# A two-layer linear-attention and MLP kernel: q and k of a token tile as one product of 1280 columns, G in two wide parts, block moves a tile ahead

## The chip, the core and the metric

The kernel runs on one core of one Trainium2 chip, in one launch. The metric is the device time of that launch in microseconds (us), the median of several runs. The engines named below are TensorE (PE in the profile; its weight loads are PEld), VectorE (DVE), ScalarE (ACT), GpSimd (POOL) and SyncE (SP, which issues the transfers).

## The reference

All data are float32: 2048 tokens of 640 features, 32 heads of 20. Two layers with the same weights follow each other; each is a linear attention block and an MLP block with squared relu (640 to 1728 to 640).

```python
def _A_ref(x, wqkv, wo):
    qkv = (x @ wqkv).reshape(B, S, 3, H, Dh).transpose(2, 0, 3, 1, 4)
    q, k, v = qkv[0], qkv[1], qkv[2]
    phi = lambda t: jnp.where(t > 0, t + 1, jnp.exp(t)) + 1e-6
    pq, pk = phi(q), phi(k)
    kv = jnp.einsum("bhsd,bhse->bhde", pk, v)
    z = jnp.einsum("bhsd->bhd", pk)
    num = jnp.einsum("bhqd,bhde->bhqe", pq, kv)
    den = jnp.einsum("bhqd,bhd->bhq", pq, z)[..., None] + 1e-6
    return (num / den).transpose(0, 2, 1, 3).reshape(B, S, D) @ wo

x = x + _A_ref(_layernorm(x), A_wqkv, A_wo)
x = x + _B_ref(_layernorm(x), B_w1, B_b1, B_w2, B_b2)   # h = relu(x w1 + b1)^2; h w2 + b2
# and both lines once more
```

## The kernel before

Tokens are handled in 16 tiles of 128 (NT = 16). Features are cut into five chunks of 128 (DC = 5). A product in float32 accuracy is made of three matmuls (`mm3`): each operand is kept as a rounded high half and a low half, and high x low, low x high and high x high are added in PSUM. `split` makes the halves: ScalarE copies the high half (an operation of 640 columns), VectorE subtracts for the low half.

The attention block of a layer first runs a loop over the 16 token tiles. v is never formed: instead G = x^T phi(k), a 640 x 640 sum over all tokens, is collected, and the kv of the heads follows as wv^T G. For tile t the loop does this:

- `proj(psk, ...)` makes k: for each of five feature chunks and each half of the 640 columns three matmuls of 320 columns, 30 in all. q is made in the same way (`q_psum`).
- the statistics and the normalisation of tile t + 2 (`a_stats`, `a_apply`; VectorE, with two small GpSimd operations), then `blocks_T`, a VectorE transpose within 32 x 32 blocks, into y.
- `blocks_move`: 16 ScalarE copies of 32 x 160 move the blocks of y into z, which is the transposed tile; `xT_split` makes the halves of z. TensorE needs them for the next tile's k.
- `phi_psum`: ScalarE's exp and relu out of PSUM; `phi_sum`: VectorE's min and add. For k the result r is split (`kh`) and GpSimd adds it to acc. The normalised tile is split as well (`xh`). For q the result is stored to DRAM by `q_store` at the start of the next tile.
- `g_chunk`: G of two tiles at a time, five chunks of twelve matmuls of 320 columns. Two or three chunks stand in each tile; VectorE adds each from PSUM into G.

In layer 0 the loop also splits two blocks of MLP weights a tile (`prep.split`: ScalarE the high half, GpSimd the low half), and loads and stores them. Three tiles, LATE = (6, 10, 14), skip their q, so that q runs three tiles behind at the end; the last three q are made later, among the work that leads to the MLP. The order on every engine is the order in which the program is written. PSUM is a ring of four slots of two banks (`ps2`), shared by k, q, G and transposes.

After the loop comes the joint: `psz` (the column sums acc, spread to all partitions by a product with ones), the last pair's G, wv^T G (`pskv`, masked into `kvbd` by VectorE), its product with wo (`psM`), and the first attention outputs (`pso`). VectorE prepares phi(q) of the first tiles between them: `b_den`, `b_blocks`. The MLP follows, with the attention outputs of later tiles worked in.

Of the kernel before, what the change touches and what calls it, by code (L numbers as in the profile page):

```python
# [35 lines left out]
LATE = (6, 10, 14)  # L36
N_WARM, N_WARM_2 = 30, 15
F_BUFS = 12
# [10 lines left out]
def kernel(  # L49
# [37 lines left out]
    def ftile(name):  # L87
        return tmp.tile([P, D], F32, tag="f", name=name, bufs=F_BUFS)

# [296 lines left out]
    for layer in range(N_LAYERS):  # L386
# [12 lines left out]
        pa = ExitStack()  # L399
        pp = pa.enter_context(  # L400
            tc.tile_pool(name=f"ap_{layer}", bufs=4, space=bass.MemoryType.PSUM, reuse_waits="tile")
        )

        ring = [0, 1, 2, 3]

        def ps2(name, hold=False):

            i = ring.pop(0)
            if not hold:
                ring.append(i)  # L410
            return pp.tile([P, 1024], F32, tag=f"p{i}", name=name, bufs=1)

        G = ap.tile([P, DC, D], F32, name="G", tag="G", bufs=1)
# [3 lines left out]
        def phi_psum(ps, rtile=None):  # L417

            e = ftile("e")
            nc.scalar.activation(halves_sb(e), halves(ps), AF.Exp)  # L420
            r = rtile or ap.tile([P, D], F32, tag="r", name="r", bufs=3)
            nc.scalar.activation(halves_sb(r), halves(ps), AF.Relu)
            return e, r

# [13 lines left out]
        def g_chunk(p, c):  # L438
            ps = ps2("psG")
            for t in (2 * p, 2 * p + 1):  # L440
                xs = xh[t][:, :, c * P : (c + 1) * P]
                for j in range(2):
                    s = slice(j * HD, (j + 1) * HD)
                    mm3(
                        ps[:, j * 512 : j * 512 + HD], xs[:, 0], xs[:, 1],
                        kh[t][:, 0, s], kh[t][:, 1, s], t % 2 == 0, t % 2 == 1,
                    )
            g = halves_sb(G[:, c])
            if p == 0:
                nc.vector.tensor_copy(g, halves(ps))  # L450
            else:
                nc.vector.tensor_tensor(out=g, in0=halves(ps), in1=g, op=ALU.add)  # L452

        def q_psum(t, hold=False):
            ps = ps2("psq", hold)
            proj(ps, xT[t], wk("q"))
            return ps

        def q_post(t, ps):
            e, r = phi_psum(ps)  # L460
            phi_sum(e, r)
            rq[t] = r
# [5 lines left out]
        if layer == 0:  # L468

            psw = ps2("psw", hold=True)  # L470

            def warm(n):
                for _ in range(n):
                    nc.tensor.transpose(psw[:, :P], ident, ident)
# [8 lines left out]
            a_trans(0, ps2("psT"))  # L483
# [7 lines left out]
            ring.append(0)  # L491
# [92 lines left out]
        n_q = 0  # L584
        for t in range(NT):
            q_store(n_q - 1)
            a_load(t + 3, src)
            if t == 0 and layer == 0:
# [9 lines left out]
            psk = ps2("psk")  # L598
            proj(psk, xT[t], wk("k"))
            if t + 1 in yza:  # L600
                blocks_move(yza[t + 1], range(4) if t in LATE else (0, 1))
            elif t < 2 and layer == 0:
                if t == 0:
                    psq = ps2("psq")
                    proj(psq, xT[t], wk("q"), range(3))
                a_trans(t + 1, ps2("psT"))
                if t == 0:
                    proj(psq, xT[t], wk("q"), range(3, DC))
            early = t == 0 and layer > 0
            if not early:  # L610
                a_stats(t + 2)
            first = t == 0 and layer == 0
            if first:
                a_apply(t + 2)
            if t in LATE:
                xT_split(t + 1, yza.pop(t + 1)[1])
            e, r = phi_psum(psk)
            if first:
                eq, rq[t] = phi_psum(psq)
            phi_sum(e, r)  # L620
            if t >= 2:
                for c in ((0, 1) if t % 2 == 0 else (3, 4)):
                    g_chunk((t - 2) // 2, c)
            if t + 1 in yza:
                blocks_move(yza[t + 1], (2, 3))
# [4 lines left out]
            kh[t] = split_new(r, "kh")  # L630
            if t == 0:
                nc.gpsimd.tensor_copy(acc, r)
            else:
                nc.gpsimd.tensor_tensor(out=acc, in0=acc, in1=r, op=ALU.add)
            if not first and not early:
                a_apply(t + 2)
            if t + 2 < NT and not first and not early:
                yza[t + 2] = blocks_T(xt[t + 2])
            if t not in LATE:
                if not first:  # L640
                    psq = q_psum(n_q)
                if layer == 0:
                    first_loads.step(1 if t else 0, 1)
                if first:
                    phi_sum(eq, rq[t])
                else:
                    q_post(n_q, psq)
                n_q += 1
            if layer == 0 and t >= 1:
                if t > 1 and t not in LATE:  # L650
                    prep.split()
                    prep.split()
                if t + 1 not in LATE:
                    prep.load()
                    prep.load()
            if t >= 2 and t % 2 == 0:
                g_chunk((t - 2) // 2, 2)
        q_store(n_q - 1)


        psz = ps2("psz")
# [7 lines left out]
        b_den(0)  # L669
        b_blocks(0)  # L670
        blocks_move(yzp[0], range(4))
        for c in range(DC):
            g_chunk(NT // 2 - 1, c)
            if c == 1:
                b_den(1)
                b_blocks(1)
            if c == 3:
                b_den(2)
        b_split(0, xtile("pT"))
        blocks_move(yzp[1], range(3))  # L680
        psq = q_psum(NT - 3, hold=True)
        q_slot = ({0, 1, 2, 3} - set(ring)).pop()

# [8 lines left out]
        for c in range(NH):  # L692
            n = head_rows(c)
            ps = ps2("pskv")
            for d in range(DC):
                nc.tensor.matmul(  # L696
                    ps[:n, :n], vo["v", d][:, HR * c : HR * c + n], G[:, d, HR * c : HR * c + n],
                    start=d == 0, stop=d == DC - 1,
                )
            nc.vector.tensor_tensor(  # L700
                out=kvbd[c][:n, P : P + n], in0=ps[:n, :n], in1=maskf[:n, :n], op=ALU.mult
            )
            if c == 0:
                blocks_move(yzp[1], (3,))
                e, rl = phi_psum(psq)
                b_load_pq(3)
            if c == 1:
                b_div(2)
                b_load_x(0)
            if c == 2:  # L710
                yzp[2] = blocks_T(pq.pop(2))
            if c == 3:
                b_split(1, xtile("pT"))
                b_load_x(1)
            if c == NH - 1:
                phi_sum(e, rl)
                nc.sync.dma_start(pqd[NT - 3], rl)
                ring.append(q_slot)
# [62 lines left out]
        proj(psq, xT[NT - 2], wk("q"))  # L781
# [6 lines left out]
        proj(psq, xT[NT - 1], wk("q"))  # L788
        phi_sum(eq2, rl2)
        nc.sync.dma_start(pqd[NT - 2], rl2)  # L790
# [277 lines left out]
        for g in range(NG):  # L1068
            for c in range(NF):
# [23 lines left out]
                if g == 0 and c == 0:  # L1093
                    phi_sum(*last_q)
                    nc.sync.dma_start(pqd[NT - 1], last_q[1])
# [36 lines left out]
```

## Time and profile before

| | before |
|---|---|
| runs | 1376.4, 1376.06, 1375.82 us (median 1376.06) |
| profiled execution | 1375.58 us, its span 1373.8 us |
| TensorE matmuls | 1363.1 us busy, 7440 records |
| ScalarE, VectorE, GpSimd | 784.9, 857.5, 142.8 us busy |
| loop over the tiles, layer 0 | from 8.8 to 205.3 us |
| joint, layer 0 (psz to the last psM) | from 205.3 to 237.4 us |
| loop and joint, layer 1 | from 692.1 to 883.1 and to 915.2 us |

The span runs from the first to the last instruction of the profiled execution. Busy time of TensorE is modelled and overlaps at the ends; what a matmul costs in a stream is read from the distance of starts. A bracket behind a row tells how long the engine stood idle before it and what ended that.

### The profile page before, as it was taken

To read this page: it belongs to the slowest core of one execution; us is meant where nothing else is said; L and a number is where in the kernel's file an instruction comes from. 1 tells how busy PE (TensorE), PEld (TensorE's weight loads), DVE (VectorE), ACT (ScalarE), POOL (GpSimd) and SP (SyncE) were. 2 spreads that over 40 slices of the span, in tenths; PEclk is the share of its full clock that TensorE was granted. 3 is DMA by queue.
4 is the path that set the end of the run, shared out by engine and by line. 5 is a ranking of instruction groups with operands and counts; after the bars stand their busy time and mean duration, and the time that the engine had idled before them with its cause. 6 is when DMAs were issued, how large, how long until landed. Compare 5 with 4: busy or idle time off the path is not lost. (4 is left out here: it accounts for less than half of the span.)

```text
span 1373.8 us, 19815 instructions
## 1 busy us (share of the span) xinstructions
PE 1363.1 (99%) x7440; PEld 1219.6 (89%) x7440; DVE 857.5 (62%) x1375; ACT 784.9 (57%) x1893; POOL 142.8 (10%) x196
## 2 busy tenths in 40 slices
PE   9999999999999999999999999999999999999998
PEld 8999998988888888888899999988888888888887
DVE  7868768687575566443466767677866655753423
ACT  5978867666456464421457778586764663563110
POOL 2434330000000000000011122100000000000000
PEclk9999999999999999999999999999999999999999
DMA  5555574372562373275421022345635535623622
GB/s 182 191 193 197 192 240 168 111 255 100 197 232 88 125 269 114 79 273 195 175 103 58 30 68 78 115 163 180 213 106 199 185 97 192 237 86 114 234 85 96
DMA packets 79434, 213.48 MB, mean 155 GB/s; under 512 B 9962, under 2 KB 21738, under 8 KB 78698
## 3 DMA queue, kind: packets, MB, share of 16 engines
q1 hardware_dynamic: 79194, 212.01, 45.2%
q8 instruction: 59, 0.97, 0.3%
q14 instruction: 37, 0.30, 0.1%
q10 hardware_dynamic: 144, 0.20, 0.0%
HBM read 162.70 MB, written 49.48 MB: 154 GB/s over the span
## 5 line engine op out<-in xcount | busy, mean ns | idle before, releaser
L319 ACT ACTIVATE z<-y 32x160 f32<-32x160 f32 x1424 | 476.2, 334 | 139.6 <-DVE y L310 120.8
L849 ACT ACTIVATE hr<-psh,b1sb 128x512 f32<-128x512 f32 x102 | 70.3, 690 | 311.6 <-PE psh L837 310.9
L837 PE MATMUL psh<-xTb,u 128*128 128x512 f32 x1010 | 241.3, 390 | 0.0
L837 PEld LDWEIGHTS psh<-xTb,u 128*128 128x128 f32 x1010 | 188.4, 188 | 38.6 <-ACT hr L849 0.3
L850 DVE TENSOR_TENSOR hr<-hr 128x512 f32<-128x512 f32 x104 | 71.0, 683 | 235.9 <-ACT hr L849 235.9
L887 PE MATMUL psa<-u,h 128*128 128x512 f32 x832 | 200.9, 390 | 0.0
L887 PEld LDWEIGHTS psa<-u,h 128*128 128x128 f32 x832 | 156.0, 188 | 33.0 <-DVE h L852 0.7
L333 PE MATMUL psk<-kq,xT 128*128 128x320 f32 x960 | 148.1, 310 | 3.8 <-DVE xT L94 1.8
L333 PE MATMUL psq<-kq,xT 128*128 128x320 f32 x960 | 146.7, 309 | 1.1 <-DVE kq L94 1.1
L333 PEld LDWEIGHTS psk<-kq,xT 128*128 128x128 f32 x960 | 142.0, 188 | 6.3 <-DVE xT L94 2.9
L333 PE MATMUL psG<-kh,xh 128*128 128x320 f32 x960 | 147.5, 309 | 0.0
L333 PE MATMUL pso<-uM,pT 128*128 128x320 f32 x960 | 145.1, 309 | 0.0
L333 PEld LDWEIGHTS pso<-uM,pT 128*128 128x128 f32 x960 | 142.6, 188 | 2.8 <-DVE uM L94 0.9
L333 PEld LDWEIGHTS psq<-kq,xT 128*128 128x128 f32 x960 | 142.0, 188 | 1.3 <-DVE kq L94 1.3
L837 PE MATMUL psh<-xTb,uw 128*128 128x512 f32 x600 | 142.8, 389 | 0.0
L333 PEld LDWEIGHTS psG<-kh,xh 128*128 128x128 f32 x960 | 142.4, 188 | 0.3
L837 PEld LDWEIGHTS psh<-xTb,uw 128*128 128x128 f32 x600 | 112.2, 188 | 22.7
L887 PE MATMUL psa<-uw,h 128*128 128x512 f32 x480 | 115.3, 389 | 0.0
L294 POOL TENSOR_SCALAR rs<-mv 128x1 f32<-128x1 f32 x64 | 15.2, 238 | 933.5 <-DVE mv L292 933.5
L887 PEld LDWEIGHTS psa<-uw,h 128*128 128x128 f32 x480 | 90.1, 188 | 18.7
L852 DVE TENSOR_TENSOR h<-hr,h 128x512 fp32r<-128x512 f32 x104 | 72.0, 692 | 3.6
L565 DVE TENSOR_TENSOR xr<-pso,xr 128x640 f32<-128x640 f32 x32 | 26.2, 820 | 64.2 <-PE pso L333 63.9
(94 smaller groups left out, 1375.6 us busy)
## 6 DMA issues: line engine op xcount, KB each, us to landing
u<-kept_w SPq DMA_DIRECT2D x136, 640.0 KB, 4.3
x<-x SPq DMA_DIRECT2D x48, 320.0 KB, 5.7
kept_w<-uprep SPq DMA_DIRECT2D x17, 640.0 KB, 4.4
pqt<-pq SPq DMA_DIRECT2D x32, 320.0 KB, 5.0
x<-xr SPq DMA_DIRECT2D x32, 320.0 KB, 4.6
pq<-r SPq DMA_DIRECT2D x28, 320.0 KB, 2.3
kept_kq<-kq SPq DMA_DIRECT2D x10, 640.0 KB, 6.3
x<-in_B_w_dram SPq DMA_DIRECT2D x20, 320.0 KB, 4.6
```

The source lines that it names most:

```text
L294: nc.gpsimd.tensor_scalar(rs, mv[:, 1:2], LN_EPS, None, op0=ALU.add)
L319: nc.scalar.activation(zv[j * B32 : (j + 1) * B32, :, i, :], yv[i * B32 : (i + 1) * B32, :, j, :], AF.Copy)
L333: nc.tensor.matmul(ps, a, b, start=first and i == 0, stop=last and i == 2)
L565: nc.vector.tensor_tensor(out=v, in0=halves(ps), in1=v, op=ALU.add)
L837: nc.tensor.matmul(ps, a[:, d, :], bb[:, d, :], start=d == 0 and i == 0, stop=d == DC - 1 and i == len(seq) - 1,)
L849: nc.scalar.activation(r, ps, AF.Relu, bias=b1sb[:, c : c + 1])
L850: nc.vector.tensor_tensor(out=r, in0=r, in1=r, op=ALU.mult)
L852: nc.vector.tensor_tensor(out=h[:, 1], in0=r, in1=h[:, 0].bitcast(F32), op=ALU.subtract)
L887: nc.tensor.matmul(ps, l, r, start=first and k == 0, stop=last and k == len(a) - 1)
```

## The change

Seven edits go together.

- **k and q are one product.** The weights of k and q lie side by side (1280 columns), and `kq_bank` makes 512, 512 and 256 of them into three banks, 15 matmuls each. k is columns 0 to 639, so k's exp and relu can begin after the second bank; q is in two pieces (384 and 256 columns) and its exp and relu take two operations each (`phi_parts`). They are written at the start of the next tile (`q_post(t - 1)`), its min and add after that tile's statistics (`q_sum`), its store a tile later. The first tile of layer 0 and the late tiles keep halves of 320.
- **G is 640 x 512, and its last 128 columns are kept transposed.** `g_unit` makes five units of 512 columns and two of 320 (G's strip, transposed, in `GT`) for two tiles: four in the even tile, three in the odd one. After the last pair the strip is turned by five TensorE transposes into `Gs`, and wv^T G is made in two parts where a group of heads crosses column 512.
- **Half of a tile's block moves stand a tile earlier:** `move(t + 2, AHEAD)` at the end of tile t, the other half after the first bank of tile t + 1.
- **PSUM in the loop** is split by use: two slots of two banks for k and q, two single banks for the rest of q, two single banks for G. The old ring is opened after the loop.
- **LATE** is (9, 13, 15) instead of (6, 10, 14); the weight splits of layer 0 stand in tiles 2 to 9 and 11, ahead of `xT_split`.
- **The r buffers** are two instead of three.
- **The joint** is written in another order: half of the first late q before psz, the rest after G; `b_blocks(1)` and `b_den(2)` stand later.

```diff
-LATE = (6, 10, 14)
+LATE = (9, 13, 15)
+AHEAD = 2
...
-            r = rtile or ap.tile([P, D], F32, tag="r", name="r", bufs=3)
-            nc.scalar.activation(halves_sb(r), halves(ps), AF.Relu)
+            r = rtile or ap.tile([P, D], F32, tag="r", name="r", bufs=2)
+            for f, v in parts:
+                nc.scalar.activation(f(e), v, AF.Exp)
+            for f, v in parts:
+                nc.scalar.activation(f(r), v, AF.Relu)
             return e, r
...
+        def g_unit(p, i, ps):
+            if i < DC:
+                n, g = DM, G[:, i]
+                ls, rs = slice(i * P, (i + 1) * P), slice(0, DM)
+                left, right = xh, kh
+            else:
+                n = HD
+                ls, rs = slice(DM, D), slice((i - DC) * HD, (i - DC + 1) * HD)
+                left, right, g = kh, xh, GT_[:, rs]
             for t in (2 * p, 2 * p + 1):
+                a, b = left[t][:, :, ls], right[t][:, :, rs]
+                mm3(ps[:, :n], a[:, 0], a[:, 1], b[:, 0], b[:, 1], t % 2 == 0, t % 2 == 1)
...
+        def kq_bank(t, ps, b):
+            s = slice(b * 512, min(b * 512 + 512, 2 * D))
+            a = xT[t]
+            for c in range(DC):
+                mm3(
+                    ps, a[:, 0, c, :], a[:, 1, c, :],
+                    kq[c][:, 0, s], kq[c][:, 1, s], c == 0, c == DC - 1,
+                )
...
         for t in range(NT):
...
+            q_post(t - 1)
+            ps = ps_kq(t)
...
+            late = t in LATE
+            if late:
+                proj(ps, xT[t], wk("k"), range(3))
+            else:
+                kq_bank(t, ps[:, :512], 0)
+            move(t + 1)
             if not early:
                 a_stats(t + 2)
+            q_sum(t - 1)
...
+                a_apply(t + 2)
+                yza[t + 2] = blocks_T(xt[t + 2])
+            unit()
+            if layer == 0:
+                if 2 <= t < 10 or t == 11:
+                    prep.split()
+                    prep.split()
...
             if t + 1 in yza:
                 xT_split(t + 1, yza.pop(t + 1)[1])
...
             xh[t] = split_new(xt[t], "xh")
+            if late:
+                proj(ps, xT[t], wk("k"), range(3, DC))
             else:
+                kq_bank(t, ps[:, 512:], 1)
+            e, r = phi_psum(ps) if late else phi_flat(ps[:, :D])
+            if late or t in (2, 6):
+                unit()
+            phi_sum(e, r)
+            unit()
+            k_post(t, r)
+            if not late:
+                psb = ps_q(t)
+                kq_bank(t, psb[:, : 2 * D - 1024], 2)
+                held[t] = ps, psb
+            while units:
+                unit()
+            move(t + 2, AHEAD)
...
+        late_half(0)
         psz = ps2("psz")
...
+        for i in (5, 6, 0, 1, 2, 3, 4):
+            g_unit(NT // 2 - 1, i, ps2("psG"))
+            if i == 0:
+                psT = ps2("psT")
+                transpose5(psT, GT_)
+                Gs = ap.tile([P, DC, P], F32, tag="r", name="Gs", bufs=2)
...
+                b_den(0)
+            if i == 1:
+                b_blocks(0)
+                blocks_move(yzp[0], range(4))
+            if i == 3:
+                b_den(1)
+        late_half(1)
+        b_blocks(1)
```

More of the change, by code (lines that the diff above doesn't have):

```diff
@@ L449, in g_chunk @@
             if p == 0:
-                nc.vector.tensor_copy(g, halves(ps))
+                nc.vector.tensor_copy(g, ps[:, :n])
             else:
[L452 to L462, printed above, removed]
+                nc.vector.tensor_tensor(out=g, in0=ps[:, :n], in1=g, op=ALU.add)
@@ L468 @@
         if layer == 0:
-            psw = ps2("psw", hold=True)
+            psw = ps_kq(0)
             def warm(n):
@@ L582, in f_split, with k_post, move @@
             split(u[:, 0], u[:, 1], sv)
-        n_q = 0
+        def k_post(t, r):
+            kh[t] = split_new(r, "kh")
+            if t == 0:
+                nc.gpsimd.tensor_copy(acc, r)
+            else:
+                nc.gpsimd.tensor_tensor(out=acc, in0=acc, in1=r, op=ALU.add)
+        moved = {}
+        def move(t, n=P // B32):
+            if t in yza:
+                blocks_move(yza[t], range(moved.get(t, 0), n))
+                moved[t] = n
         for t in range(NT):
-            q_store(n_q - 1)
+            first = t == 0 and layer == 0
+            early = t == 0 and layer > 0
+            q_store(t - 2)
             a_load(t + 3, src)
-            if t == 0 and layer == 0:
+            if first:
                 late_consts()
@@ L597 @@
                 load_vo(2 * t - 25)
[L598 to L608, printed above, removed]
@@ L609, with unit @@
-            early = t == 0 and layer > 0
+            units = []
+            if t >= 2:
+                units = [0, 1, 2, 3] if t % 2 == 0 else [4, 5, 6]
+            def unit():
+                if units:
+                    i = units.pop(0)
+                    g_unit(t // 2 - 1, i, ps_g(i))
+            q_post(t - 1)
+            ps = ps_kq(t)
+            if first:
+                proj(ps, xT[t], wk("k"))
+                e, r = phi_psum(ps)
+                phi_sum(e, r)
+                pq0 = [ps_q(0), ps_g(0)]
+                wq = wk("q")
+                for c in range(DC):
+                    for j in range(2):
+                        s = slice(j * HD, (j + 1) * HD)
+                        mm3(
+                            pq0[j][:, :HD], xT[t][:, 0, c, :], xT[t][:, 1, c, :],
+                            wq[c][:, 0, s], wq[c][:, 1, s], c == 0, c == DC - 1,
+                        )
+                    if c == 2:
+                        a_trans(1, ps_kq(1))
+                        a_stats(2)
+                        a_apply(2)
+                xh[t] = split_new(xt[t], "xh")
+                k_post(t, r)
+                e, rq[t] = phi_parts(
+                    [(lambda a, j=j: a[:, j * HD : (j + 1) * HD], pq0[j][:, :HD]) for j in range(2)]
+                )
+                phi_sum(e, rq[t])
+                continue
@@ L617 @@
[L617 to L623, printed above, removed]
+                yza[t + 2] = blocks_T(xt[t + 2])
[4 more added lines that the diff above has]
+                    prep.split()
+                if 1 <= t < 9 or t == 10:
+                    prep.load()
+                    prep.load()
@@ L629 @@
             xh[t] = split_new(xt[t], "xh")
-            kh[t] = split_new(r, "kh")
-            if t == 0:
-                nc.gpsimd.tensor_copy(acc, r)
-            else:
[L634 to L648, printed above, removed]
@@ new lines, with ps2 @@
+        q_store(NT - 1)
+        pka.close()
+        pp = pa.enter_context(
+            tc.tile_pool(name=f"ap_{layer}", bufs=4, space=bass.MemoryType.PSUM, reuse_waits="tile")
+        )
+        ring = [0, 1, 2, 3] if layer == 0 else [3, 2, 1, 0]
+        def ps2(name, hold=False):
+            i = ring.pop(0)
+            if not hold:
+                ring.append(i)
+            if i in early_slots:
+                return early_slots.pop(i)
+            return pp.tile([P, 1024], F32, tag=f"p{i}", name=name, bufs=1)
@@ new lines, with late_half @@
+        early_slots = {}
+        if layer > 0:
+            early_slots = {
+                i: pp.tile([P, 1024], F32, tag=f"p{i}", name=f"ps{i}", bufs=1) for i in range(4)
+            }
+        psq = ps2("psq", hold=True)
+        q_slot = ({0, 1, 2, 3} - set(ring)).pop()
+        wq = wk("q")
+        def late_half(j):
+            s = slice(j * HD, (j + 1) * HD)
+            for c in range(DC):
+                mm3(
+                    psq[:, j * 512 : j * 512 + HD], xT[LATE[0]][:, 0, c, :], xT[LATE[0]][:, 1, c, :],
+                    wq[c][:, 0, s], wq[c][:, 1, s], c == 0, c == DC - 1,
+                )
@@ L668 @@
         nc.scalar.activation(halves_sb(zbc), halves(psz), AF.Copy)
[L669 to L674, printed above, removed]
-                b_den(1)
[L676 to L682, printed above, removed]
+        for i in (5, 6, 0, 1, 2, 3, 4):
[4 more added lines that the diff above has]
+                Gs = ap.tile([P, DC, P], F32, tag="r", name="Gs", bufs=2)
+                nc.scalar.activation(
+                    Gs, psT[:, :D].rearrange("p (c n) -> p c n", c=DC), AF.Copy
+                )
+                b_den(0)
[3 more added lines that the diff above has]
+            if i == 3:
+                b_den(1)
+        late_half(1)
+        b_blocks(1)
         kvbd = []
@@ L694 @@
             ps = ps2("pskv")
[L695 to L698, printed above, removed]
-                )
-            nc.vector.tensor_tensor(
-                out=kvbd[c][:n, P : P + n], in0=ps[:n, :n], in1=maskf[:n, :n], op=ALU.mult
-            )
+            o, m = HR * c, max(min(DM - HR * c, n), 0)
+            parts = [
+                v for v in ((0, m, 0, G, o), (m, n, 512, Gs, max(o - DM, 0))) if v[0] < v[1]
+            ]
+            for q0, q1, b, g, w0 in parts:
+                for d in range(DC):
+                    nc.tensor.matmul(
+                        ps[:n, b : b + q1 - q0], vo["v", d][:, o : o + n],
+                        g[:, d, w0 : w0 + q1 - q0], start=d == 0, stop=d == DC - 1,
+                    )
+            for q0, q1, b, g, w0 in parts:
+                nc.vector.tensor_tensor(
+                    out=kvbd[c][:n, P + q0 : P + q1], in0=ps[:n, b : b + q1 - q0],
+                    in1=maskf[:n, q0:q1], op=ALU.mult,
+                )
             if c == 0:
-                blocks_move(yzp[1], (3,))
-                e, rl = phi_psum(psq)
+                b_split(0, xtile("pT"))
+                blocks_move(yzp[1], range(3))
                 b_load_pq(3)
             if c == 1:
-                b_div(2)
                 b_load_x(0)
             if c == 2:
-                yzp[2] = blocks_T(pq.pop(2))
+                b_den(2)
+                e, rl = phi_psum(psq, ftile("rl"))
             if c == 3:
-                b_split(1, xtile("pT"))
+                blocks_move(yzp[1], (3,))
                 b_load_x(1)
             if c == NH - 1:
+                b_blocks(2)
+                b_split(1, xtile("pT"))
                 phi_sum(e, rl)
-                nc.sync.dma_start(pqd[NT - 3], rl)
+                nc.sync.dma_start(pqd[LATE[0]], rl)
                 ring.append(q_slot)
```

96 lines of the change are left out of this document (54 added, 42 removed).

## The prediction

> **What bounds the kernel now.** I read the page first, for the engine that carries the span, then the waits of TensorE, for what is left to win by order alone.
>
> ```profile
> span 1373.8 us, 19815 instructions
> PE 1363.1 (99%) x7440; PEld 1219.6 (89%) x7440; DVE 857.5 (62%) x1375; ACT 784.9 (57%) x1893; POOL 142.8 (10%) x196
> PEclk9999999999999999999999999999999999999999
> PE psk L333 <- DVE xT L94: 1.8, 4, 0.5
> PE psw L474 <- POOL ident masks.py:199: 1.4, 1, 1.4
> PE psk L333 <- ACT xT L93: 1.2, 2, 0.6
> PE psq L333 <- DVE kq L94: 1.1, 1, 1.1
> PE psk L333 <- ACT r L422: 0.8, 2, 0.4
> PE pskv L696 <- DVE G L452: 0.4, 2, 0.2
> ```
>
> TensorE is busy 99% of the span at full clock, and all its waits (columns: microseconds, times, longest) come to some 7 us. So a change counts by the TensorE time it removes and by the waits it makes. Of the waits, 3.8 us (the three psk rows) stand in the loop over token tiles, which is rewritten; 2.5 us at the start are left alone.
>
> What a matmul costs is read from the chain that ended last, where TensorE runs without a gap (columns: start, us, what):
>
> ```profile
> 848.97 4.40 PE psk L333 x30
> 898.58 5.17 PE pskv L696 x52
> 903.76 11.55 PE psM L734 x40
> 937.50 1.09 PE psT L304 x10
> 953.22 3.40 PE psh L837 x15
> ```
>
> 30 matmuls of 320 columns take 4.40 us, 146.7 ns each; 15 of 512 take 3.40 us, 226.7 ns. The difference, 80 ns for 192 columns, is 0.417 ns a column, and 13.3 ns are left over in both: a matmul costs 13.3 ns plus its columns. The same columns in fewer matmuls cost less.
>
> **Part 1: q and k as one product.** Before: 60 matmuls of 320 a tile, 8.80 us. After: 30 of 512 (6.80 us) and 15 of 256. No row shows 256 columns in this form. The line gives 13.3 + 106.7 = 120 ns (an estimate); from below the psT row bounds it, 109 ns for a pair of weight load and 128 columns; from above the 320-column row, 146.7 ns. I take 120, since the line goes through two rows of the very instruction. That is 1.80 us, 8.60 in all, 0.20 us less a tile. The first tile of layer 0 and the three late tiles of each layer keep 320 columns: 12 + 13 = 25 tiles, **-5.0 us**. The bounds for 375 narrow matmuls are -4.1 and +10.0 us around that.
>
> [...]
>
> **Part 2: G.** Before: 60 matmuls of 320 for two tiles, 8.80 us. After: five units of six at 512 (6.80) and two of six at 320 (1.76), 8.56 us. 0.24 us less for each of 16 pairs, **-3.84 us**.
>
> **Part 3: what the transposed strip adds.** Five transposes a layer at 109 ns: 0.55 us, **+1.1** in both. The product with v is split where the strip begins: per layer 5 of 30 products of 120 columns become 5 of 32 and 5 of 88.
>
> ```profile
> 223.78 2.14 PE L696 MATMUL pskv<-G,uraw 128*120 128x120 f32 x24
> 225.85 1.07 PE L734 MATMUL psM<-uraw,kvbd 120*128 120x320 f32 x3
> ```
>
> A product has two records; 52 records take 5.17 us, about 100 ns each. The last 24, 14 of 120 columns and 10 of 40, take 2.07 us up to the next row; less 14 x 100 that leaves 67 ns for a narrow one. So 10 x 67 + 10 x about 85 (between 67 and 100) - 10 x 100 = 0.5 us, **+1.0** in both; at worst 2.0 (all at 100), at best 0.7.
>
> **Part 4: waits in the loop.** The 3.8 us of the old loop go with it: they follow its late tiles, as here in layer 0, where a tile without q gave ScalarE too little time for all 16 block moves, and the next tiles start late:
>
> ```profile
> 92.23 4.66 PE L333 MATMUL psk<-kq,xT 128*128 128x320 f32 x30 [0.38 <-ACT r L422]
> 105.43 0.42 PE L333 MATMUL psk<-kq,xT 128*128 128x320 f32 x1 [0.63 <-ACT xT L93]
> 106.29 4.52 PE L333 MATMUL psk<-kq,xT 128*128 128x320 f32 x29 [0.44 <-DVE xT L94]
> ```
>
> Now half of the moves go a tile ahead. What comes in their place I walk by hand in a layer 0 tile, where ScalarE also splits two weight blocks (uprep):
>
> ```profile
> 57.05 1.36 ACT L194 ACTIVATE uprep<-st 128x640 fp32r<-128x640 f32 x2
> 58.30 2.76 ACT L319 ACTIVATE z<-y 32x160 f32<-32x160 f32 x8
> 61.08 0.70 ACT L420 ACTIVATE e<-psk 128x640 f32<-128x640 f32 x1
> 61.69 0.70 ACT L422 ACTIVATE r<-psk 128x640 f32<-128x640 f32 x1
> 65.19 0.74 ACT L93 ACTIVATE xT<-z 128x640 fp32r<-128x640 f32 x1
> 65.84 0.72 ACT L93 ACTIVATE xh<-xt 128x640 fp32r<-128x640 f32 x1
> 66.47 0.73 ACT L93 ACTIVATE kh<-r 128x640 fp32r<-128x640 f32 x1
> L194 ACT ACTIVATE uprep<-st 128x320 fp32r<-128x320 f32 x1 | 0.5, 464 | 0.0
> 58.33 2.02 DVE L428 TENSOR_TENSOR r<-e,r 128x640 f32<-128x640 f32 x1
> 69.59 0.45 DVE L427 TENSOR_SCALAR e<-e 128x640 f32<-128x640 f32 x1
> 70.15 0.83 DVE L428 TENSOR_TENSOR r<-e,r 128x640 f32<-128x640 f32 x1
> 690.59 2.48 DVE L912 TENSOR_TENSOR x<-psa,x 128x512 f32<-128x512 f32 x4 [1.29 <-PE psa L887]
> ```
>
> From start to start an operation of 640 takes ScalarE 0.63 us, eight moves 2.75, two splits 1.25. q's exp and relu come in four pieces (384 and 256 wide): the 320-wide row's 464 ns, some 0.36 from start to start, gives about 1.4 us against 1.2. TensorE's tile, with 0 at its start: first bank to 3.4, a G unit to 4.76, second bank to 8.16, then G and q to 14.04 (even) or 11.72 (odd). ScalarE in an even tile that it enters 2.0 us late: q to 3.4, moves to 6.15, splits to 7.4, xT to 8.05, xh to 8.7, k's exp and relu to 9.9, a wait of 0.9 for VectorE's min and add, kh to 11.45, moves a tile ahead to 14.2. It is 0.2 us late into the odd tile: 1.6, 4.35, 5.6, 6.25, 6.9; k is ready at 8.16, so 9.4; kh to 10.9, moves to 13.7, again 2.0 late. A closed cycle: xT with VectorE's low half is done by 9, and TensorE wants it at 11.72 or 14.04. A late tile lasts 7.52 us: entered 0.2 late, xT's low half is there at 6.25 + 0.83 = 7.1, 0.4 us ahead. Layer 1 has no weight splits, 1.25 us more room.
>
> What is late next is VectorE. G has two single banks, and the fourth unit of an even tile, at 12.68, needs the second one emptied; that emptying (512 columns, 0.62 us by the psa row) is queued behind the add at some 10.9, so done at 11.5. Where POOL works on VectorE's side an add takes 2.02 instead of 0.83 us, and the unit waits about half a microsecond. I put 0.5 on each of layer 0's four even tiles with weight splits, and 0.2 for xT of tile 1, now queued behind k's min and add: **-3.8 + 2.2**; bounds 0 and 6 for the new waits.
>
> **Part 5: waits at the joint.** The product of ones with acc now follows k of the last tile by two G units and half a q, 3.96 us, where there were 7.9 (3.52 of G, 4.40 of q).
>
> ```profile
> 875.37 3.52 PE psG L333 x24
> 199.88 1.58 POOL L634 TENSOR_TENSOR acc<-acc,r 128x640 f32<-128x640 f32 x1 [5.01 <-DVE r L428]
> 885.40 0.83 DVE pr L536
> 886.25 0.83 DVE den L538
> 887.11 0.19 DVE den L544
> 887.32 0.36 DVE den L545
> 887.71 0.84 DVE pqt L547
> 888.57 0.84 DVE y L310
> pq<-r SPq DMA_DIRECT2D x28, 320.0 KB, 2.3
> ```
>
> Exp 0.6, a G emptying until 1.4 after k, min and add to 2.7, POOL's sum 1.6: 4.3, so a wait of 0.4. Further on VectorE has b_blocks(1) (0.19, 0.36, 0.84 and 0.84, 2.2 us) ahead of the first kvbd, which frees the slot for the fourth pskv: by the same walk some 0.3. For two layers +1.4, less the 0.4 of pskv now: **+1.0** (bounds -0.4 and +4).
>
> **The sum.** -5.0 - 3.84 + 1.1 + 1.0 - 3.8 + 2.2 + 1.0 = -7.3 us. The profiled execution took 1375.58 us, 1.8 beyond its span: 1368.2. The median of the three runs, 1376.06, is 0.5 above it, so I say **1368.7 us**.
>
> **The rivals.**
>
> *ScalarE's queue doesn't close* (chance 0.12). If the wait before kh is 2.1 us (the add at 2.02) in every tile with weight splits, such a tile costs ScalarE 11.4 + 2.1 = 13.5 us against TensorE's mean of 12.88: 0.6 us in each of eight tiles, and about 1 at the late tile 9, which still has splits. 6 us in place of 2.2: 1372.5, up to 1375 with the joint at its bound. For it: a cover of only 0.4 us at tile 9. Against: ScalarE's waits for PE are there to be filled.
>
> *The 256-column matmul doesn't run at the line's pace* (0.09); this one ends on the other side. All 375 stand on TensorE's path. From 120 + 7.3/0.375 = 139 ns on the gain is gone. At the 320 columns' 146.7 ns it costs 10.0 us: 1378.7. At the pace of the full-precision psM row, 578 ns a product of 320 columns, so 462 for 256, it would be 128 us: about 1497. For it: no row has this width. Against: the 128-column transposes pass at 109 ns.
>
> *Fewer matmuls save nothing* (0.05): the 13.3 ns belong to something that isn't there per matmul. Then parts 1 and 2 give 0: 1377.5. Against: both rows agree on it. [...]
>
> *q's relu waits for a store* (0.03). The r buffers go from three to two, and the relu of q must wait until the row of q before it is in DRAM. The store is issued a few microseconds into a tile and wanted some 9 us later; it lands in 2.3. Past 13 us (ScalarE's 4 us of cover included) each excess counts in some 22 tiles: 0.7 us of it would mean 1384.
>
> That the change doesn't do what it says is out: the built order holds the 512- and 256-column matmuls as counted.
>
> **How the numbers follow.** The forecast has 0.71. 0.2%, about what a measurement of this kernel can tell from no change, is 2.8 us: 1373.3 to 1378.8. The forecast lies on the fast side, the ScalarE rival two thirds (0.08); faster 0.79. Same: the rest of it 0.04, a third of the narrow rival 0.03, the third rival 0.05, so 0.12. Slower: 0.06 and 0.03, so 0.09. The forecast's own range is 1364 (no new waits at all is 1365.1, and a narrow matmul a little under the line takes the rest) to 1373; with the ScalarE rival to 1375.5, which leaves out some 2 in 10.
>
> **What would show it.** Right: rows of 512 columns at 15 in 3.40 us, of 256 at 15 in 1.80; the psk waits for xT gone; a new wait for G's emptying (VectorE) in layer 0's even tiles and one for acc before psz. Wrong: 256-column rows spaced over 139 ns; TensorE waiting for ScalarE at each tile start of layer 0; ScalarE waiting for a DMA before q's relu; or a joint with more than 2 us of waits a layer.

## The result, and the profile after

The change makes the kernel slower: 1382.21 us (median of six runs, 1381.84 to 1382.36) against 1375.89 us for the kernel before in the same session, a ratio of 1.0045 with a 95% interval of [1.0032, 1.0058]. The forecast was 1368.7 us.

From the page of the kernel after, first the span and the engines, then TensorE's list of waits (microseconds in all, times, longest):

```profile
span 1380.3 us, 18631 instructions
PE 1363.2 (99%) x6807; PEld 1168.7 (85%) x6807; DVE 884.6 (64%) x1409; ACT 789.8 (57%) x1947; POOL 148.5 (11%) x196
PE psG L334 <- DVE G L481: 4.9, 2, 2.5
PE psG L334 <- DVE G L479: 2.2, 1, 2.2
PE psG L334 <- DVE GT L481: 1.2, 1, 1.2
PE psG L334 <- DVE kh L95: 0.8, 1, 0.8
PE ps L779 <- POOL acc L634: 0.5, 1, 0.5
PE psz L779 <- POOL acc L634: 0.5, 1, 0.5
```

There are 633 matmul records fewer, and TensorE is as long busy as before (1363.2 against 1363.1 us). Against the psk waits of before (3.8 us) stand 9.1 us of waits for VectorE in the tile loop, 8.3 of them for the emptying of G.

The saving itself arrived. TensorE's timeline of the kernel after, tile 6 and the start of tile 7 of layer 0, a stretch without a wait:

```profile
89.91 3.59 PE L334 MATMUL pskq<-kq,xT 128*128 128x512 f32 x15
93.33 1.52 PE L334 MATMUL psG<-kh,xh 128*128 128x512 f32 x6
...
100.81 1.96 PE L334 MATMUL psq<-kq,xT 128*128 128x256 f32 x15
102.60 1.55 PE L334 MATMUL psG<-kh,xh 128*128 128x512 f32 x6
103.99 2.20 PE L334 MATMUL pskq<-kq,xT 128*128 128x512 f32 x9
```

From start to start 15 of 512 columns take 3.42 us and 15 of 256 take 1.79; the tile takes 14.08. Layer 1 shows the gain whole: from the first product of k to the first pso it takes 219.6 us (702.16 to 921.77) where it took 223.1. Layer 0 takes 238.45 us (9.03 to 247.48) where it took 228.6. So the loss is one of layer 0 alone, 9.8 us, and what most of layer 0's tiles have and layer 1's haven't is two weight blocks that are loaded, split and stored.

Tile 4 of layer 0 in the kernel after, all engines (start, us, and the idle time before a row with its releaser):

```profile
67.91 1.37 ACT L195 ACTIVATE uprep<-st 128x640 fp32r<-128x640 f32 x2
68.73 3.68 POOL L199 TENSOR_TENSOR uprep<-st,uprep 128x640 fp32r<-128x640 f32 x2 [3.67 <-ACT uprep L195]
69.94 1.04 DVE L95 TENSOR_TENSOR xT<-z,xT 128x640 fp32r<-128x640 f32 x1 [2.00 <-ACT xT L94]
70.91 2.19 DVE L95 TENSOR_TENSOR xh<-xt,xh 128x640 fp32r<-128x640 f32 x1
73.02 0.48 DVE L453 TENSOR_SCALAR e<-e 128x640 f32<-128x640 f32 x1
73.60 0.83 DVE L454 TENSOR_TENSOR r<-e,r 128x640 f32<-128x640 f32 x1
74.34 0.68 DVE L481 TENSOR_TENSOR G<-psG,G 128x512 f32<-128x512 f32 x1
74.46 0.74 ACT L94 ACTIVATE kh<-r 128x640 fp32r<-128x640 f32 x1 [2.75 <-DVE r L454]
75.08 2.15 PE L334 MATMUL psG<-kh,xh 128*128 128x512 f32 x6 [2.48 <-DVE G L481]
```

GpSimd computes the low halves of the two weight blocks from 68.73 to 72.41. VectorE's subtraction for xh, 0.82 us in the kernel before, takes 2.19 and ends at 73.10, 0.69 us after GpSimd has done. Behind it in VectorE's queue stand min, add and the emptying of G's bank. So ScalarE waits 2.75 us before kh, and TensorE 2.48 us for the bank.

The windows of the same profile show a second effect, the granted clock (PEclk) behind the three longest waits and, in the third row, behind one of 1.21 us:

```profile
core 0: us, PE busy (x) PEld busy (x) DVE busy (x) ACT busy (x) POOL busy (x), PEclk, DMA share, GB/s
45.70:48.70 3.00, 3.00 (x8) 2.30 (x7) 2.80 (x4) 2.60 (x7) 1.56 (x1) 0.50 0.97 381
76.00:79.00 3.00, 3.00 (x9) 2.32 (x8) 2.97 (x7) 2.92 (x10) 0.06 (x1) 0.50 0.67 222
120.40:123.40 3.00, 2.90 (x13) 2.40 (x14) 2.32 (x7) 2.90 (x10) 0.89 (x2) 1.00 0.88 229
134.50:137.50 3.00, 3.00 (x14) 3.00 (x12) 2.88 (x7) 2.91 (x9) 0.86 (x2) 0.51 0.15 61
```

After pauses of 2.20, 2.48 and 2.47 us TensorE runs for about 3.4 us at half clock, and each such stretch costs it some 1.7 us more (an estimate: half of 3.4).

### The profile page after: what moved, and what is told of

It is laid out like the page before. It is cut to its first block, busy times and chain, and to the rows that moved or that the text cites. A ratio compares the mean times of both kernels' runs of the same rounds, so it can differ in the third digit from the quotient of the medians.

```text
span 1380.3 us, 18631 instructions
## 1 busy us (share of the span) xinstructions
PE 1363.2 (99%) x6807; PEld 1168.7 (85%) x6807; DVE 884.6 (64%) x1409; ACT 789.8 (57%) x1947; POOL 148.5 (11%) x196
## 5 line engine op out<-in xcount | busy, mean ns | idle before, releaser
L334 PE MATMUL pskq<-kq,xT 128*128 128x512 f32 (+1 forms) x960 | 215.1, 377 | 0.3 <-DVE xT L95 0.2
L334 PEld LDWEIGHTS pskq<-kq,xT 128*128 128x128 f32 x960 | 174.8, 191 | 31.0 <-DVE xT L95 0.4
L334 PE MATMUL psG<-kh,xh 128*128 128x512 f32 x468 | 119.4, 396 | 9.3 <-DVE G L481 4.9
L334 PEld LDWEIGHTS psG<-kh,xh 128*128 128x128 f32 x468 | 86.5, 189 | 28.6 <-DVE G L481 5.8
L334 PE MATMUL psq<-kq,xT 128*128 128x256 f32 (+1 forms) x540 | 75.2, 291 | 0.9 <-DVE kq L95 0.9
L334 PEld LDWEIGHTS psq<-kq,xT 128*128 128x128 f32 x540 | 72.5, 190 | 2.5 <-DVE kq L95 1.1
```

Source lines behind the costliest of these rows:

```text
L334: nc.tensor.matmul(ps, a, b, start=first and i == 0, stop=last and i == 2)
```

## The experiments

**The theory: a ring.** In layer 0 ScalarE's work goes in a circle that its own queue closes: kh 0.65 us, the moves a tile ahead 2.77, q's exp and relu 1.45, moves 2.78, the first weight split 0.8, then GpSimd's 3.7 for the low halves, for which VectorE's xh waits, xh itself 0.65, min 0.6, add 0.85, and kh again. That is some 14.2 us, and TensorE's tile is 12.88 on average. Tiles 2 to 9, eight in a row, have such splits, and tile 11. In tile 4, between the starts of kh at 60.25 and 74.46, the 2.75 us before kh are the only wait of ScalarE that the timeline shows: its queue goes round without slack. The timeline shows kh of tile 1 and of tile 9 at:

```profile
31.29 0.74 ACT L94 ACTIVATE kh<-r 128x640 fp32r<-128x640 f32 x1 [2.32 <-DVE r L454]
...
145.86 0.74 ACT L94 ACTIVATE kh<-r 128x640 fp32r<-128x640 f32 x1 [2.73 <-DVE r L454]
```

114.6 us for eight tiles, 14.3 each. The rivals were that the pauses cost by the half clock, that VectorE's order (min and add ahead of the emptying) is what counts, and that the splits harm only what stands right behind them.

**The splits back at the end of the tile.** In the kernel before, the splits stood behind q; the change put them ahead of xT.

```diff
             unit()
-            if layer == 0:
-                if 2 <= t < 10 or t == 11:
-                    prep.split()
-                    prep.split()
-                if 1 <= t < 9 or t == 10:
-                    prep.load()
-                    prep.load()
             if t + 1 in yza:
                 xT_split(t + 1, yza.pop(t + 1)[1])
...
             while units:
                 unit()
+            if layer == 0:
+                if 2 <= t < 10 or t == 11:
+                    prep.split()
+                    prep.split()
+                if 1 <= t < 9 or t == 10:
+                    prep.load()
+                    prep.load()
             move(t + 2, AHEAD)
```

> The weight splits and loads of layer 0 stand at the end of a tile, ahead of its block moves, instead of ahead of the split of xT; all else as in the changed kernel. Theory 1 (GpSimd's low halves, 3.66 us for two, hold up VectorE's subtractions for xT and xh, so the second G bank is emptied late): VectorE's xh subtraction falls from 2.16 to about 0.82 us, the waits of TensorE for G in layer 0 (8.3 us) and the half-clock stretches behind them (3 of 3.4 us) go: 1367 to 1371 us. Theory 2 (the emptying is late because it is queued behind k's min and add, whoever else runs): the waits stay at over 1 us in tiles 2, 4 and 8, and the time at over 1377.

Measured: 1369.8 us, ratio to before 0.9956 [0.994, 0.9973]. In the timeline of this kernel, around tile 4:

```profile
56.76 1.35 ACT L195 ACTIVATE uprep<-st 128x640 fp32r<-128x640 f32 x2
57.70 3.69 POOL L199 TENSOR_TENSOR uprep<-st,uprep 128x640 fp32r<-128x640 f32 x2
58.02 2.75 ACT L320 ACTIVATE z<-y 32x160 f32<-32x160 f32 x8
66.55 0.82 DVE L95 TENSOR_TENSOR xh<-xt,xh 128x640 fp32r<-128x640 f32 x1
68.72 0.74 ACT L94 ACTIVATE kh<-r 128x640 fp32r<-128x640 f32 x1 [1.14 <-DVE r L454]
```

The low halves take as long as before, but now beside the block moves, where VectorE's queue holds nothing that waits for them for long. xh takes 0.82 again, kh follows kh after 12.6 us (56.12 to 68.72), and the longest wait for G is 0.7 us. The order of everything else is as in the changed kernel (the loads of later blocks move with the splits), so this one place made it slower: it is worth 12.4 us.

**No low halves.** To see that it is GpSimd's part and not ScalarE's, the low halves became constants, at the same place.

```diff
-                split_low(nm, c, u, raw, eng=nc.gpsimd)
+                nc.gpsimd.memset(unit_parts(nm, c, u, raw)[1].bitcast(F32), 0.0)
```

> The splits stay where the change put them, but the low halves of the weights prepared in layer 0 are zeros (a GpSimd fill that reads nothing), so those low halves are left out of the MLP's result. Theory 1: xh's subtraction at about 0.82 us, no wait of TensorE for G above 1 us, clock 1.0 throughout: 1366 to 1370 us. Theory 2: waits for G above 1 us in tiles 2, 4 and 8 remain: above 1376 us.

Measured: 1370.11 us in one run. xh takes 0.82 us, kh follows kh after 12.6. ScalarE's two splits are still ahead of xT, and so are the loads, so it isn't they that hurt.

**The pause filled.** Eighteen transposes ahead of the fourth G unit of tiles 2, 4 and 8, into a bank that is free, keep TensorE busy where it paused.

```diff
             while units:
+                if layer == 0 and t in (2, 4, 8) and len(units) == 1:
+                    for _ in range(18):
+                        nc.tensor.transpose(psb[:, 256:384], ident, ident)
                 unit()
```

> The changed kernel with 18 transposes of 128 columns (about 1.96 us, into a part of q's bank that nobody reads) just ahead of the fourth G unit of tiles 2, 4 and 8 of layer 0, where TensorE stood idle for 2.2 to 2.5 us. If the half clock follows from TensorE's idleness: the three stretches at clock 0.5 go, 1.7 us each, 1376.5 to 1378 us with VectorE as late as before. If the half clock has another cause: 1382 us, with the stretches still there.

Measured: 1382.25 us, ratio 1.0048 [1.0033, 1.0063]: the expectation missed. The clock is full where it had been half, as the windows of this kernel say:

```profile
45.70:48.70 3.00, 3.00 (x15) 2.45 (x14) 2.79 (x4) 2.37 (x7) 1.57 (x1) 1.00 0.98 384
76.00:79.00 3.00, 3.00 (x15) 2.47 (x14) 2.97 (x5) 2.91 (x10) 0.30 (x1) 1.00 0.73 233
```

So the half clock came with the pauses (1.00 with the pause filled, 0.50 without), and yet the clock costs nothing here: with the faster matmuls TensorE arrives sooner and waits elsewhere, as in tile 4:

```profile
63.23 0.96 PE L334 MATMUL psG<-kh,xh 128*128 128x512 f32 x3 [1.42 <-DVE GT L479]
```

That speaks for a bound that lies outside TensorE, and against the rival of the half clock.

**The bank emptied ahead of min and add.** Tiles 2 and 6 of the change do that; here 4 and 8 do too.

```diff
-            if late or t in (2, 6):
+            if late or t in (2, 4, 6, 8):
                 unit()
```

> In tiles 4 and 8, as in 2 and 6, VectorE empties the second G bank ahead of k's min and add. Theory 1: xh's subtraction stays at 2.16 us, but the emptying comes 1.2 us earlier: the waits in tiles 4 and 8 fall from 2.48 to about 1.2 us and, if it takes a pause of about 2 us to lower the clock, two half-clock stretches go as well: about 1376 us. If tile 2, which has this order already and still waits 2.2 us, is the rule, no wait falls by more than 0.4 us: 1381 us.

Measured: 1383.83 us in one run, where the expectation was a gain. In tiles 4 and 8 the wait for the bank falls to 1.18 us each, but kh comes 0.6 later (14.81 us from tile 3's to tile 4's), by the emptying that now stands in the ring, and other waits appear (two of 1.45 and 1.47 us for GT). What helps TensorE at one place lengthens the ring.

**The splits a few lines further down.** The same block stands behind xh's split here, ahead of k's exp, min, add and kh.

```diff
             xh[t] = split_new(xt[t], "xh")
+            if layer == 0:
+                if 2 <= t < 10 or t == 11:
+                    prep.split()
+                    prep.split()
...
```

> The changed kernel with the two weight splits of layer 0's tiles moved by a few lines only: from ahead of xT's and xh's splits to just behind them, still ahead of k's exp, min, add and kh. Theory 1 (a ring: kh, moves a tile ahead, q's exp and relu, moves, weight splits, GpSimd's two low halves, and what VectorE must do before kh; the ring is longer than TensorE's 12.88 us a tile): GpSimd's 3.7 us now stand before k's add in place of xh's subtraction, kh waits for that add as before. From the start of kh: 0.64 + 2.77 + 1.45 + 2.78 + 1.3 (xT, xh) + 0.7 + 3.7 + 0.8 (add) = about 14.1 us from kh to kh; xh low takes 0.82 again, the two-input add of k grows to 2 us or more, and the time stays at 1379 to 1383. Rival (the harm is done at xT and xh: the splits delay the two operands that TensorE wants next): with xT and xh free the ring is no matter, 1368 to 1372.

Measured: 1378.65 us, ratio 1.0023 [1.0013, 1.0032], 0.35 below the range of the ring and far from the rival's. The timeline of tile 4:

```profile
68.66 0.82 DVE L95 TENSOR_TENSOR xh<-xt,xh 128x640 fp32r<-128x640 f32 x1
69.22 3.48 POOL L199 TENSOR_TENSOR uprep<-st,uprep 128x640 fp32r<-128x640 f32 x2 [4.98 <-ACT uprep L195]
70.39 0.88 DVE L453 TENSOR_SCALAR e<-e 128x640 f32<-128x640 f32 x1 [0.91 <-ACT e L443]
71.37 2.01 DVE L454 TENSOR_TENSOR r<-e,r 128x640 f32<-128x640 f32 x1
73.42 0.74 ACT L94 ACTIVATE kh<-r 128x640 fp32r<-128x640 f32 x1 [2.47 <-DVE r L454]
```

xT and xh are free, and now the add, the next VectorE operation with two inputs, takes 2.01 us. The min, with one input, took longer too, 0.88 us instead of 0.48. Both places between the moves and kh that were tried put GpSimd's low halves into the ring; this one makes it 13.93 us (59.49 to 73.42).

**One low half of two.** Every first low half is a constant, every second one is computed.

```diff
+                self.odd = not getattr(self, "odd", False)
+                if self.odd:
+                    nc.gpsimd.memset(unit_parts(nm, c, u, raw)[1].bitcast(F32), 0.0)
+                else:
+                    split_low(nm, c, u, raw, eng=nc.gpsimd)
```

> The changed kernel, where GpSimd fills the first of every two low halves of the weight blocks in layer 0 with zeros (0.6 us) and computes the second as before; this leaves out one half of that computation. Theory 1 (a ring against TensorE's tile, so a cost only above 12.88 us): GpSimd's part ends about 1.2 us sooner (the one subtraction can start only after the second split), so the ring is about 13.0 us, 0.1 over TensorE in eight tiles: 1370 to 1373; the waits for G's emptying fall under 1.5 us. Rival (each low half costs its time, wherever TensorE stands): half of the cost goes, 12.4 of which 6 remain: 1375 to 1377.

Measured: 1376.04 us, ratio 1.0001 [0.9991, 1.001], in the rival's range and not in the ring's. The timeline tells whether the theory or its arithmetic was off:

```profile
68.36 1.58 POOL L199 TENSOR_TENSOR uprep<-st,uprep 128x640 fp32r<-128x640 f32 x1 [3.75 <-ACT uprep L195]
68.94 1.68 DVE L95 TENSOR_TENSOR xT<-z,xT 128x640 fp32r<-128x640 f32 x1 [1.99 <-ACT xT L94]
70.55 0.81 DVE L95 TENSOR_TENSOR xh<-xt,xh 128x640 fp32r<-128x640 f32 x1
```

The one subtraction ends at 69.94, and xT, which passed between two GpSimd operations in the changed kernel (1.04 us), waits for its end; xh comes after that. From kh to kh it is 13.46 us (59.27 to 72.73), not the 13.0 that I had worked out. Time and ring agree, as the next table shows; what missed was the length of the ring, so this run alone doesn't refute the rival. The splits at the end of the tile do, where both low halves are computed and the time is that of the kernel without them (1369.8 and 1370.11 us); whether at the old place the cost sets in only above a threshold, as the ring has it, this run leaves open.

**The ring against the time.** kh of tile 1 and of tile 9, read in each profile's timeline as above, and the kernel's time (of a single run in the first and the sixth row):

| kernel | kh, tile 1 to tile 9 | eight tiles, us | time, us | difference |
|---|---|---|---|---|
| bank emptied first | 31.65 to 147.34 | 115.69 | 1383.83 | 1268.14 |
| the change | 31.29 to 145.86 | 114.57 | 1382.21 | 1267.64 |
| pause filled | 31.51 to 146.03 | 114.52 | 1382.25 | 1267.73 |
| splits behind xh | 31.66 to 142.34 | 110.68 | 1378.65 | 1267.97 |
| one low half | 31.79 to 140.01 | 108.22 | 1376.04 | 1267.82 |
| no low halves | 31.57 to 133.79 | 102.22 | 1370.11 | 1267.89 |
| splits at the end | 31.55 to 132.87 | 101.32 | 1369.8 | 1268.48 |

Over 14 us of times the difference stays within 0.9 us. What these kernels differ by is the pace of kh in eight tiles, almost microsecond for microsecond. That says where the time goes, and not by itself what sets the pace, since any delay in these tiles would lengthen the stretch; for the ring speak ScalarE's queue without slack and the filled pause, whose TensorE has its clock back and whose kh keeps its pace (114.52 against 114.57 us). In the last two rows the ring is the shorter of the two, and the pace is TensorE's own.

**The place alone, in the old loop.** The kernel before, with its splits moved to the place that the change gave them.

```diff
                 blocks_move(yza[t + 1], (2, 3))
+            if layer == 0 and t >= 1:
+                if t > 1 and t not in LATE:
+                    prep.split()
+                    prep.split()
...
+            if t + 1 in yza:
                 xT_split(t + 1, yza.pop(t + 1)[1])
```

> The kernel before with one thing of the change alone: its weight splits of layer 0 stand ahead of xT's split, behind the second half of the block moves. Theory 1 (the place of the splits makes a ring also in the old loop): moves 2.75, split 0.7, GpSimd 3.7, xh low 0.8, kh low 0.8, apply 0.6, y 0.85, moves 2.75, k's exp and relu 1.3 = 14.3 us against a tile of 13.2, some 1 us in each of up to eight tiles less what slack takes at the late tiles: 1379 to 1385, with xh low at about 2.2 us. Rival (only the new order hurts, where kh waits behind moves and q on ScalarE): the old loop has nothing waiting behind kh, so 1375 to 1377.

Measured: 1402.33 us, ratio 1.0193 [1.0179, 1.0208]: slower, as the theory had it, but by 26.5 us and not 3 to 9. The timeline of two tiles:

```profile
66.39 2.77 ACT L319 ACTIVATE z<-y 32x160 f32<-32x160 f32 x8 [4.31 <-DVE y L310]
...
76.29 2.20 DVE L94 TENSOR_TENSOR xh<-xt,xh 128x640 fp32r<-128x640 f32 x1
77.77 2.16 POOL L642 TENSOR_TENSOR acc<-acc,r 128x640 f32<-128x640 f32 x1
78.42 2.19 DVE L94 TENSOR_TENSOR kh<-r,kh 128x640 fp32r<-128x640 f32 x1
...
82.11 2.77 ACT L319 ACTIVATE z<-y 32x160 f32<-32x160 f32 x8 [4.38 <-DVE y L310]
```

The old loop's ring goes through y, the next tile's transpose, for which ScalarE waits 4.3 us with its moves. I had put 0.8 for kh's subtraction; it takes 2.19, because GpSimd's acc, next in its queue behind the low halves, gets in ahead of it. So this ring is 15.7 us (66.39 to 82.11), not 14.3. From kh of tile 1 to kh of tile 5 this loop takes 60.71 us (30.82 to 91.53), the kernel before 49.54 (30.18 to 79.72): 2.8 us more in each of four tiles, and nine tiles have splits. The place harms both loops, and the old one more.

**The product with acc two units later.** On top of the splits at the end of the tile, psz stands behind G units 5 and 6 of the last pair.

```diff
-        psz = ps2("psz")
...
         for i in (5, 6, 0, 1, 2, 3, 4):
             g_unit(NT // 2 - 1, i, ps2("psG"))
+            if i == 6:
+                psz = ps2("psz")
...
```

> The changed kernel with the weight splits at the end of the tile (as in e1_splits_late, 1369.8 us) and the product of ones with acc two units of G later at the joint of each layer. Theory: in e1 TensorE waits 0.47 us for acc in both layers; with two units of 0.88 us ahead these waits go and nothing else becomes late, so 0.9 us less: 1368.5 to 1369.3. Rival: zbc, made from that product, is then late for the denominators, and VectorE's work for the first block, or the pskv products, wait in its place: 1369.5 to 1371.

Measured: 1369.83 us, ratio 0.9956 [0.9943, 0.9969], no gain over 1369.8. TensorE's timeline:

```profile
204.23 1.44 PE L334 MATMUL psG<-xh,kh 128*128 128x320 f32 x8 [0.59 <-DVE kh L95]
205.50 1.24 PE L782 MATMUL psz<-acc,ones 128*128 128x320 f32 x4
```

The wait for acc is gone, and unit 5 waits 0.59 us for the last tile's kh instead. The wait was one for the last tile's k, whichever of its uses comes first. That was neither of the two ways expected.

The version to keep is the change with the splits at the end of the tile: it beats the kernel before by 0.44% (0.27 to 0.6%) and the change by 12.4 us.

## Why the prediction was wrong

**Parts 1 and 2, right.** 256 columns run at the line's pace (1.79 us for 15 where 1.80 was forecast), the even tile takes 14.08 us (14.04), the odd one 11.71 (11.72). The rivals on the matmul's price are out.

**Part 3, mis-sized by 1.3 us.** The products with v now take 7.24 us a layer (228.69 to 235.93), where they took 6.11 without their wait: +2.3 in both layers, where +1.0 was forecast and 2.0 was the bound. The groups of the kernel after, in this stretch:

```profile
L822 PE MATMUL pskv<-G,uraw 128*120 128x120 f32 x40 | 4.4, 268 | 0.0
L822 PE MATMUL pskv<-G,uraw 128*120 128x32 f32 x10 | 1.2, 271 | 0.1
L822 PE MATMUL pskv<-Gs,uraw 128*40 128x40 f32 x10 | 0.6, 210 | 0.0
```

A product of 32 columns costs here what one of 120 costs (271 and 268 ns a record in these groups): 120 columns of weights (the 128*120) are loaded for both. With 40 columns of weights a record took 210. The cheap 67 ns that I had read from the row of 40 columns belonged to its 40 columns of weights. And the 100 ns were a mean over 42 records with 120 columns of weights and 10 with 40, so too low for the ten records a layer that came in addition: at 111 ns they are 1.1 us a layer. The trace has 50 records with 120 columns of weights in 5.54 us (228.69 to 234.23), 111 ns each.

**Part 4, wrong: the step that failed.** The walk through ScalarE's tile gave "a wait of 0.9 for VectorE's min and add" before kh, and so a closed cycle. The wait measured is 2.7 to 3.3 us in all but one of the tiles 2 to 9; with the splits at the end of the tile it is 1.14 in tile 4. The walk had placed the weight splits' ScalarE part at their new place, and not the GpSimd part that follows from it, nor the VectorE operations (xT's and xh's low halves) that stand between it and min. It had the sign that would have led there: the add of 2.02 us beside POOL, quoted from the profile before. I took it as a price for one add and put half a microsecond on four tiles; as a wait it falls here on xh's subtraction (2.19 us), on which ScalarE's whole tile hangs. Instead of +2.2 us for layer 0's new waits the place of the splits cost 12.4.

**The rival "ScalarE's queue doesn't close"** was the right one in kind. Its wait of 2.1 us, its 13.5 us per tile and its 6 us were too small, because it too thought of the add alone, one operation's wait and not the end of both low halves: measured, 14.2 to 14.8 us a tile (13.9 for the last, which ends in the late tile 9). The change then ends outside the range, and on the slow side, where I had put nothing of that rival.

**Part 5, right for acc.** The wait for acc is 0.47 us in each layer; 0.4 was forecast. The 0.3 us a layer that VectorE's b_blocks(1) was to cost the fourth pskv didn't come: TensorE's list has no such wait. So the part is +0.5 and not +1.0.

**The sum, without the ring.** With the splits at the end of the tile the kernel takes 1369.8 us, and its new waits in layer 0's loop come to 1.8 (0.9 for G, 0.7 for kh, 0.2 for xT), where 2.2 were forecast. The forecast of 1368.7, plus the 1.3 us of part 3 and less the 0.5 of part 5, is 1369.5. So the other terms hold together, and part 4's place of the splits is the error.

## What to carry to other kernels

When a step is moved, walk every engine's share of it to the new place, and look at what is queued there on the engines it collides with; a ScalarE copy of 1.3 us brought 3.7 us of GpSimd with it. A loop in which an engine waits for what it has itself delayed has a period of its own: add the ring up from an operation to its next occurrence, and compare it with the bound engine's tile. If a wait is taken away and the time stays, look for the ring's operation and measure its pace, as kh was measured here.

## What the runs showed of the hardware

VectorE's operations with two inputs outside PSUM took longer where they met a GpSimd subtraction, and in these timelines they ended 0.68 or 0.69 us after its end: xh in tile 4 of the changed kernel took 2.19 us in place of 0.82 (to 73.10, GpSimd to 72.41), the add in the kernel with the splits behind xh 2.01 in place of 0.83 (to 73.38, GpSimd to 72.70), and with one low half instead of two the operation that met it, xT, 1.68 (to 70.62, GpSimd to 69.94). The min, with a single input, took longer as well: 0.88 us in tile 4 of the kernel with the splits behind xh, where GpSimd's two subtractions ran from 69.22 to 72.70, against 0.48 otherwise. The emptying of G, which has one input in PSUM, didn't: in tile 5 of the changed kernel it took 0.69 us (83.15 to 83.84) beside two such subtractions (82.93 to 86.62). It goes both ways: acc, 1.58 us (median) in the kernel before, took 2.16 beside VectorE in the old loop with early splits (77.77 to 79.93). In a run of two GpSimd operations one VectorE operation got in between: in tile 4 of the changed kernel xT (1.04 us) ended at 70.98, 0.68 us after the first of them (68.73 to 70.30), and xh 0.69 us after the second (70.26 to 72.41). What lies behind these times the runs don't show.

TensorE's granted clock fell to half after pauses in the tile loop: in the changed kernel after 2.20, 2.48 and 2.47 us (0.50, 0.50 and 0.51 in the windows above), in the kernel with the splits behind xh after 2.75 and 2.15 us (a mean of 0.60 from 62.3 to 65.3 and of 0.71 from 129.9 to 132.9), and in the old loop with early splits also behind one of 1.90 us (0.54 from 105.3 to 108), and not behind one of 1.80 (1.00 from 165.2 to 168); there it fell once more, behind two pauses of 1.54 and 0.91 us within 3 us (0.50 from 180.6 to 184). Before that I had counted on full clock throughout. In the kernel after, each of the three stretches at half clock lasts about 3.4 us; in windows of 1 us from 44.7 on the clock of the first is 0.80, 0.50, 0.50, 0.50 and 0.99. Whether the length of a pause alone decides, and whether it depends on when the pause falls, these few pauses don't settle.
